# Output projection as seven Strassen block products at the end of a two-attention kernel

## The chip, the cores and the metric

The kernel runs on one core of one Trainium2 chip. The metric is the device time of one execution in microseconds (us). Matmuls run on TensorE (PE), with weight loads as instructions of their own (PEld); elementwise work on VectorE (DVE), ScalarE (ACT) and GpSimd (POOL). DMAs are issued from the queues of SyncE (SP), ACT and POOL.

## The reference

Two attention layers with inputs of their own, A and B, are computed, and their outputs are put side by side. Each has x of 2048 x 1024, wqkv of 1024 x 3072, wo of 1024 x 1024, and 32 heads of 32.

```python
def _A_ref(x, wqkv, wo):      # a query sees 8 keys, 2 positions apart
    W, dil = 8, 2
    idx = pos[:, None] - (jnp.arange(W) * dil)[None, :]
    ...
    attn = _softmax(jnp.where(idx >= 0, logits, -1e9), axis=-1)
    o = jnp.einsum("bhsw,bhswd->bhsd", attn, vg)
    return o.transpose(0, 2, 1, 3).reshape(B, S, D) @ wo

def _B_ref(x, wqkv, wo):      # a query sees the last 256 keys
    scores = jnp.einsum("bhqd,bhkd->bhqk", q, k) * (Dh ** -0.5)
    mask = (idx[:, None] - idx[None, :] >= 0) & (idx[:, None] - idx[None, :] < 256)
    p = _softmax(jnp.where(mask[None, None], scores, -1e9), axis=-1)
    o = jnp.einsum("bhqk,bhkd->bhqd", p, v)
    return o.transpose(0, 2, 1, 3).reshape(B, S, D) @ wo

return jnp.concatenate([a, b], axis=-1)
```

## The kernel before

The work is cut into 8 units of 512 rows: four of B ("dense" units, 0 to 3), then four of A ("window" units, 4 to 7; A's even and odd rows are separated first, so that its dilated window becomes 8 neighbours). A unit has 8 head groups of 4 heads. Units 0, 4 and 6 begin a sequence; the others have a halo of keys from the unit before.

All products keep fp32 accuracy by splitting each operand into a high part (a cast to fp32r) and a low part (what the cast left), and adding three matmuls, high x high, high x low and low x high (`TERMS`). The class `Stream` holds the list of operands that come from DRAM (`items`), 512 KB each: a raw tile is loaded on the POOL queue (`load_to`, L159), cast on DVE or ACT (L201, L204) and its low part made on DVE (L207) by `split_to`. There are `NRAW` raw tiles.

The products run as one ordered list, `gemm`: for each head group the queries and keys (`qk_items`, L518), at certain groups a part of V (`v_items`, L583), at the groups 2 to 5 of a unit the output projection of the unit before (`o_items`, L645, two column blocks of 128 per group), and at the end the projection of unit 7. One column block is 8 x 3 matmuls of 128x512 into one of three PSUM tiles; the result goes out through one staging tile `ost` and ACT's queue.

The attention of a dense head group goes as follows. Queries and keys are copied out of PSUM into `nat` (L455, L459), and SP copies them into one of two stacks, `qst` and `kst` (L479), with the halo from DRAM (L408); the stack of group g is filled again for group g + 2 after the last matmul that reads it. The first pass has 16 score matmuls (L857), each followed by a masked maximum on DVE (L862) and an exponential with its sum on ACT (L867). The logarithms of the sums and the maxima are put into the stack as additional rows (L880 to L902). The second pass has the transposed scores (L940), the exponential (L947), masks on POOL or DVE (L926, L929), and the products with V (L987). The first pass of a group runs between the instructions of the second pass of the group before. A window group has one pass (L711 to L774). In the end `finish` (L822, L826) copies a group's output out of PSUM as a high and a low part; ten such tiles (`NO`) wait for the projection.

The order of the instructions is fixed when the kernel is built: a planner with a clock of its own (`Clock`) gives each instruction of DVE, ACT, POOL and SP a duration, and at each step puts the item on PE that can start first, the second pass ahead of the first and both ahead of `gemm`. A callback can be put off to a planned time (`ck.defer`). Every engine then runs its instructions in the planned order and waits on semaphores for what it needs.

## Time and profile before

| | |
|---|---|
| median of 3 runs | 1830.61 us (1827.76 to 1834.19) |
| profiled execution, first to last instruction | 1830.6 us |
| granted TensorE clock, mean | 0.999 |
| PE busy | 1807.8 us, 14826 matmuls |
| DVE, ACT, POOL busy | 1202.9, 889.4, 394.4 us |
| DMA | 257.43 MB, 141 GB/s in the mean |

Busy time is the time in which an engine's instructions run, without the sequencer's own (waits, DMA issues). Matmuls overlap, so their mean duration in a group's row is longer than the time that one takes from the next; that price is read from a stretch of many in a row. A group's row gives, in this order, line, engine, operation, out<-in, shapes, count, then busy time and mean ns of one, then the engine's idle time ahead of them and what ended it.

### The profile page before, as it was taken

Reading aid. Unit: us, or ns where it says so; the run is one execution under the profiler, and the core shown is the slowest. Engines: PE = TensorE matmul, PEld = TensorE weight load, DVE = VectorE, ACT = ScalarE, POOL = GpSimd, SP = SyncE. Lnnn points to the kernel's source line nnn. Section 1 sums busy time; section 2 is a strip of 40 time slices with the busy share of each in tenths; the row PEclk is TensorE's granted clock in tenths of the full one; section 3 lists DMA queues with packets and bytes.
Section 4 is the critical chain, followed back from the end, with each engine's and each line's share of the span. In section 5 each row is a group of like instructions: output and inputs, shape, how many; then the busy total and the mean of one; then the engine's idle time right before and its main releaser. Section 6 shows DMA issues by size and latency. Waiting matters only on the chain.

```text
span 1830.6 us, 38331 instructions
## 1 busy us (share of the span) xinstructions
PE 1807.8 (99%) x14826; PEld 1477.5 (81%) x14826; DVE 1202.9 (66%) x2694; ACT 889.4 (49%) x2254; POOL 394.4 (22%) x926
## 2 busy tenths in 40 slices
PE   9999999999999999999999999999999999999998
PEld 7787777888778888788887788888888788888887
DVE  6677886768867669777777564655547445655463
ACT  5556466565655655656555343433425234423331
POOL 3322323233242324332233200110001000100000
PEclk9999999999999999999999999999999999999999
DMA  8455665545656456455554343444334443534432
GB/s 242 121 138 139 176 164 150 170 121 160 164 155 164 136 151 183 125 157 141 141 142 130 110 135 116 152 143 130 119 115 143 133 138 108 162 107 128 127 104 83
DMA packets 109141, 257.43 MB, mean 141 GB/s; under 512 B 14496, under 2 KB 29856, under 8 KB 108960
## 3 DMA queue, kind: packets, MB, share of 16 engines
q0 software_dynamic: 41760, 152.06, 28.1%
q1 hardware_dynamic: 56832, 83.00, 17.6%
q10 hardware_dynamic: 10368, 19.93, 3.0%
q8 instruction: 117, 1.92, 0.5%
q14 instruction: 64, 0.52, 0.1%
HBM read 164.63 MB, written 23.07 MB: 103 GB/s over the span
## 4 chain that ended last, share of the span: by engine, by line
PE 92%; DVE 4%; DMA 2%; ACT 2%; issue 1%; SPq 0%; ACTq 0%; POOL 0%; DVEq 0%; POOLq 0%
PE g L518 37%; PE g L645 19%; PE g L583 17%; PE s L940 5%; PE s L857 5%; PE o L987 5%; PE s L711 2%; PE o L774 2%; DMA raw<-xs 1%; DVE w L207 1%; DVE s L862 1%; ACT s L867 0%; DMA qst<-nat 0%; DMA pbuf<-nat 0%; DVE x L207 0%
## 5 line engine op out<-in xcount | busy, mean ns | idle before, releaser
L518 PE MATMUL g<-x,w 128*128 128x512 f32 x3072 | 770.2, 394 | 3.8 <-DVE nm L729 2.4
L518 PEld LDWEIGHTS g<-x,w 128*128 128x128 f32 x3072 | 566.3, 189 | 114.2 <-issue 8.3
L583 PE MATMUL g<-w,x 128*128 128x256 f32 (+1 forms) x2304 | 391.9, 320 | 0.9 <-issue 0.7
L207 DVE TENSOR_TENSOR w<-raw,w 128x512 fp32r<-128x512 f32 x516 | 338.6, 698 | 52.0 <-ACT w L201 44.8
L583 PEld LDWEIGHTS g<-w,x 128*128 128x128 f32 x2304 | 332.3, 190 | 29.2 <-DVE w L207 1.8
L645 PE MATMUL g<-ot,w 128*128 128x512 f32 x1416 | 343.6, 393 | 3.7 <-DVE ot L826 1.8
L867 ACT ACTIVATE s<-s,nm 128x384 f32<-128x384 f32 (+2 forms) x512 | 274.3, 536 | 102.1 <-DVE nm L862 101.8
L862 DVE CUSTOM_DVE_ANT_0 s<-s,mask_d 128x384 f32<-128x384 f32 (+2 forms) x512 | 261.5, 553 | 88.2 <-PE s L857 87.5
L645 PEld LDWEIGHTS g<-ot,w 128*128 128x128 f32 x1416 | 262.4, 188 | 59.3 <-DVE ot L826 3.2
L926 POOL TENSOR_SCALAR_AFFINE_SELECT pbuf<-pbuf 128x128 f32<-128x128 f32 (+1 forms) x606 | 219.8, 391 | 325.1 <-ACT pbuf L947 323.8
L947 ACT ACTIVATE pbuf<-s 128x384 f32<-128x384 f32 (+2 forms) x480 | 202.7, 505 | 72.2 <-PE s L940 70.2
L159 POOL DMA_DIRECT2D raw<-wqk x126 | 68.1, 540 | 457.5 <-DVE w L207 356.3
L204 DVE CAST w<-raw 128x1024 fp32r<-128x1024 f32 x205 | 141.7, 691 | 24.8 <-PE g L518 24.0
L940 PEld LDWEIGHTS s<-qst,kst 128*128 128x128 f32 x704 | 113.0, 188 | 41.2 <-ACT s L867 16.3
L857 PE MATMUL s<-kst,qst 96*128 96x384 f32 (+2 forms) x512 | 142.4, 342 | 0.9 <-ACT s L867 0.6
L940 PE MATMUL s<-qst,kst 128*128 128x256 f32 (+2 forms) x704 | 136.5, 302 | 3.5 <-ACT s L867 3.0
L719 DVE TENSOR_TENSOR band<-s,near 128x160 f32<-128x160 f32 x128 | 32.4, 315 | 158.0 <-PE s L711 158.0
L536 ACT COPY ost<-g 128x512 f32<-128x512 f32 x54 | 31.7, 587 | 207.1 <-PE g L645 200.4
L857 PEld LDWEIGHTS s<-kst,qst 96*128 96x128 f32 x512 | 93.4, 189 | 26.2 <-issue 4.7
L826 DVE TENSOR_TENSOR ot<-o,ot 128x512 fp32r<-128x512 f32 x64 | 44.0, 688 | 101.6 <-ACT ot L822 101.4
L867 ACT ACTIVATION_READ_ACCUMULATOR s<-s,nm 128x1 f32 x512 | 105.3, 206 | 0.0
L159 POOL DMA_DIRECT2D raw<-wo x64 | 34.2, 534 | 304.2 <-DVE w L207 260.2
(77 smaller groups left out, 1298.6 us busy)
## 6 DMA issues: line engine op xcount, KB each, us to landing
raw<-wqk POOLq DMA_DIRECT2D x126, 512.0 KB, 4.3
raw<-wv POOLq DMA_DIRECT2D x72, 512.0 KB, 5.1
raw<-wo POOLq DMA_DIRECT2D x64, 512.0 KB, 4.1
qst<-nat SPq DMA_DIRECT2D x96, 256.0 KB, 5.3
kst<-nat SPq DMA_DIRECT2D x96, 256.0 KB, 5.6
raw<-xs POOLq DMA_DIRECT2D x28, 512.0 KB, 4.6
outs<-ost ACTq DMA_DIRECT2D x56, 256.0 KB, 2.3
kst<-halo SPq DMA_DIRECT2D x72, 128.0 KB, 4.5
```

The costliest lines, as they stand in the source:

```text
L159: (self.nc.scalar if early else self.nc.gpsimd).dma_start(raw if len(ap.shape) == 2 else raw.rearrange("p (a b) -> p a b", a=2), ap)
L204: nc.vector.tensor_copy(t[:, 0, :], raw)
L207: nc.vector.tensor_tensor(t[:, 1, c:c + 512], raw[:, c:c + 512], t[:, 0, c:c + 512].bitcast(F32), op=ALU.subtract)
L518: nc.tensor.matmul(h["ps"], h["w"][:, a, k * P:(k + 1) * P], xt[u][k][:, b, :], start=(k == 0 and i == 0), stop=(k == NK - 1 and i == 2))
L583: nc.tensor.matmul(ps, xt[u][kw * g + k][:, a, p0:p0 + P], h["w"][g][:, c, k], start=(first and t == 0 and half == 0), stop=(last and t == 2),
L645: nc.tensor.matmul(h["ps"], w[:, a, c:c + P], ot[u, k][:, b, :], start=(k == 0 and i == 0), stop=(k == NK - 1 and i == 2))
L857: nc.tensor.matmul(ps[:, :n], q[0:96, j, b * P:(b + 1) * P], kk[0:96, j, c0:c1], start=True, stop=True)
L862: nc.vector.tensor_tensor_reduce(ps[:, :n], ps[:, :n], mask[:, cut:full], scale=-1.0, scalar=BIG, op0=ALU.add, op1=ALU.min, accum_out=nm)
L867: nc.scalar.activation(ps[:, :n], ps[:, :n], AF.Exp, bias=nm, scale=-1.0, accum_out=sm)
L926: nc.gpsimd.affine_select(w, w, pattern=[[0, m], [step, n]], compare_op=ALU.is_ge, fill=0.0, base=base, channel_multiplier=chan)
L940: nc.tensor.matmul(ps[:, i * n:(i + 1) * n], kk[:, j, 256 + kb * P:256 + (kb + 1) * P], q[:, j, q0:q0 + n], start=True, stop=True)
L947: nc.scalar.activation(w, ps[:, :pack * n].rearrange("p (j n) -> p j n", j=pack), AF.Exp)
```

## The change

Two neighbouring units (1024 rows) and the 1024 columns are each taken as 2 x 2 blocks, and so is `wo`; the eight block products of a pair are replaced by seven (Strassen's scheme in Winograd's form). Each product is 4 column blocks of 4 x 3 matmuls. All of it stands at the end of `gemm`.

The attention output of a group no longer stays in SBUF: `finish` copies it once as fp32 into one of two tiles, and SP stores it in DRAM (`od`). The sums of blocks that Strassen needs are made by background tasks: SP loads two blocks of 512 KB into one tile, POOL makes four sums, SP stores 1 MB to DRAM (`sd` for the attention outputs, `td` for `wo`). There are 8 tasks for the two weights, from a planned time of 120 us on, and 4 for each pair after its last group; one task is planned to end before the next begins. The operands of the products are items of the stream like the others, loaded on POOL's queue; an item that needs a sum or an output is held back until the planner's clock says that it has landed (`gates`).

```diff
-NRAW, NP, NO, NS = 3, 768, 10, 4
+NRAW, NP, NS = 4, 768, 4
-O_SLOTS = {2: (0, 1), 3: (2, 3), 4: (4, 5), 5: (6, 7)}
+PRODUCTS = (("11", "11"), ("12", "21"), (0, 3), (2, 2), ("22", 1), (3, 0), (1, "22"))
+BG_FROM, BG_REST, BG_SLACK = 120.0, 8.0, 3.0
-NX, NST, NN = 9, 1, 3
+NX, NST, NN = 9, 2, 3
...
         while self.loaded < min(n, len(self.items)):
+            gate = self.gates.get(self.loaded)
+            if gate and not gate():
+                return
...
-            if u and s in O_SLOTS:
-                plan += [("o", u - 1, n) for n in O_SLOTS[s]]
...
-    plan += [("o", U - 1, n) for n in range(NG)]
+    plan += [("o", v) for v in range(U // 2)]
...
+    od = [dram.tile([P, NG, S], F32, name=f"od{u}") for u in range(U)]
+    sd = [dram.tile([P, 4, 4, S], F32, name=f"sd{v}") for v in range(U // 2)]
+    td = [dram.tile([P, 4, 4, S], F32, name=f"td{ly}") for ly in range(2)]
...
+    def o_parts(v):
+        ly = units[2 * v][0]
+        for i, (a, b) in enumerate(PRODUCTS):
+            for j in range(2):
+                key = ("o", v, i, "s", j)
+                if isinstance(a, str):
+                    u, c = 2 * v + int(a[0]) - 1, 4 * (int(a[1]) - 1) + 2 * j
+                    item(key, "xw", od[u][:, c:c + 2, :])
+                    gates[where[key]] = landed("ot", u * NG + c, u * NG + c + 1)
+                else:
+                    item(key, "xw", sd[v][:, a, 2 * j:2 * j + 2, :])
+                    gates[where[key]] = landed("s", (v, 2 * j), (v, 2 * j + 1))
+            for j in range(2):
+                key = ("o", v, i, "t", j)
+                if isinstance(b, str):
+                    n, c = 4 * (int(b[1]) - 1) + 2 * j, S * (int(b[0]) - 1)
+                    item(key, "w", wo[ly, n:n + 2, :, c:c + S].rearrange("n p c -> p n c"))
+                else:
+                    item(key, "w", td[ly][:, b, 2 * j:2 * j + 2, :])
+                    gates[where[key]] = landed("t", (ly, 2 * j), (ly, 2 * j + 1))
...
+        def run(i, n, k):
             if k == 0:
+                h["ps"], h["b"] = rg.take()
+            w, x = held["o", v, i, "t", n // 2][0], held["o", v, i, "s", k // 2][0][k % 2]
+            c = S * (n % 2) + P * k
+            for t, (a, b) in enumerate(TERMS):
+                nc.tensor.matmul(h["ps"], w[:, a, c:c + P], x[:, b, :], start=(k == 0 and t == 0),
+                                 stop=(k == 3 and t == 2))
+            if k == 1:
+                at = where["o", v, i, "t", 1] + n
+                if at < len(st.items):
+                    st.split_to(at + 1)
...
+            if i == 0:
+                h["a", n] = new("a")
+                nc.scalar.copy(h["a", n], ps)
+                e = ck.use("act", 0.485, ck.now + ck.SEM)
+            elif i == 1:
+                o = stp.tile([P, S], F32, tag="ost", name="ost")
+                e = add(o, h["a", n])
+                store(0, 0, o, e)
...
+            elif i == 5:
+                e = add(h["c", n], h["c", n])
+                store(1, 1, h["c", n], e)
+                e = add(h["a", n], h["a", n])
+            else:
+                e = add(h["a", n], h["a", n])
+                store(0, 1, h["a", n], e)
+            rg.give(bank, e)
...
+    def background():
+        if bg["busy"] or not bg["tasks"]:
+            return
+        bg["busy"] = True
+        loads, ops, dst, key, who = bg["tasks"].pop(0)
+        t = bgp.tile([P, 4, S], F32, tag="bg", name="bg")
+        for c, ap in loads:
+            if len(ap.shape) == 2:
+                ap = ap.rearrange("p (a b) -> p a b", a=2)
+            nc.sync.dma_start(t[:, c:c + 2, :], ap)
+            e = ck.copy("load", ck.now)
+        def step(n):
+            to, x, y, op = ops[n]
+            nc.gpsimd.tensor_tensor(t[:, to, :], t[:, x, :], t[:, y, :], op=op)
+            e = ck.use("pool", 1.2, ck.now)
+            ck.defer(e + BG_SLACK, (lambda: step(n + 1)) if n < 3 else finish)
+        def finish():
+            nc.sync.dma_start(dst, t)
+            e = ck.copy("load", ck.now)
+            def end():
+                done[key][who] = ck.now
+                bg["busy"] = False
+                st.load_to(st.wanted)
+                background()
+            ck.defer(e + BG_REST, end)
+        ck.defer(e + BG_SLACK, lambda: step(0))
...
+    ck.defer(BG_FROM, weight_sums)
...
     def finish(u, s, h):
-        o = opool.tile([P, 2, S], F32R, tag="ot", name="ot")
-        nc.scalar.copy(o[:, 0, :], h["o"])
...
-            nc.vector.tensor_tensor(o[:, 1, :], h["o"], o[:, 0, :].bitcast(F32), op=ALU.subtract)
...
+        o = otp.tile([P, S], F32, tag="ot", name="ot")
+        nc.scalar.copy(o, h["o"])
+        e = ck.use("act", 0.485, ck.now + ck.SEM)
+        ro.give(0, e)
+        def store():
+            nc.sync.dma_start(od[u][:, s, :], o)
+            e2 = ck.copy("store", e)
+            def end():
+                done["ot"][hg] = ck.now
+                st.load_to(st.wanted)
+                if s == NG - 1 and u % 2:
+                    output_sums(u // 2)
+            ck.defer(e2 + 1.0, end)
+        ck.defer(e, store)
```

More of the change, by code (lines that the diff above doesn't have):

```diff
@@ L139, in __init__ @@
         self.raw, self.tiles, self.ready = {}, {}, {}
[L140 removed]
+        self.loaded = self.split = self.wanted = 0
+        self.gates = {}
         self.light = light
@@ L178, in split_to @@
             self.load_to(i + 1)
+            if i not in self.raw:
+                return
             raw, t0 = self.raw.pop(i)
@@ L269, with landed @@
     unit_x(0, 2, 3)
+    od = [dram.tile([P, NG, S], F32, name=f"od{u}") for u in range(U)]
+    sd = [dram.tile([P, 4, 4, S], F32, name=f"sd{v}") for v in range(U // 2)]
+    td = [dram.tile([P, 4, 4, S], F32, name=f"td{ly}") for ly in range(2)]
+    done = {}
+    for k in ("stack", "v", "o", "ot", "nat", "second", "clear", "scores", "s", "t"):
+        done[k] = {}
+    gates = {}
+    def landed(key, *which):
+        return lambda: all(done[key].get(w, ck.now + 1) <= ck.now for w in which)
+    def o_parts(v):
[18 more added lines that the diff above has]
+                    gates[where[key]] = landed("t", (ly, 2 * j), (ly, 2 * j + 1))
     for p in plan:
@@ L354 @@
     halo = [[dram.tile([P, 2, 256], F32, name=f"halo{i}_{s}") for s in range(NG)] for i in range(2)]
-    xt, xready, ot, rows = {}, {}, {}, {}
-    done, waiting = {}, {}
-    for k in ("stack", "v", "o", "ot", "out", "nat", "second", "clear", "scores"):
-        done[k] = {}
+    xt, xready, rows, waiting = {}, {}, {}, {}
     class Ring:
@@ L764, in values_ready @@
         def values_ready():
-            if hg >= NO and ((hg - NO) // NG, NG - 1) not in done["out"]:
-                return None
             return latest(done["v"].get((u, vp)), h.get("p"), ro.when())
```

136 lines of the change are left out of this document (74 added, 62 removed).

## The prediction

> **What bounds the kernel now.** I read the head of the page and its chain first.
>
> ```profile
> span 1830.6 us, 38331 instructions
> ...
> PE 1807.8 (99%) x14826; PEld 1477.5 (81%) x14826; DVE 1202.9 (66%) x2694; ACT 889.4 (49%) x2254; POOL 394.4 (22%) x926
> ...
> PE 92%; DVE 4%; DMA 2%; ACT 2%; issue 1%; SPq 0%; ACTq 0%; POOL 0%; DVEq 0%; POOLq 0%
> ```
>
> PE is busy for 99% and 92% of the chain that ended last runs through it; no other engine passes 66%. So PE's work looks like the price of everything. But a mean over stages hides what the removed matmuls do at their place, so I asked for stretches: unit 0 in its second half, where no output projection runs yet; units 1 to 3, where it is mixed in; a stretch of the window units; the last two minutes.
>
> ```profile
> 137.80:241.90 104.10, 99.03 (x593) 77.72 (x592) 83.47 (x233) 59.19 (x189) 32.50 (x78) 1.00 0.61 165
> 245.00:1026.00 781.00, 777.63 (x4791) 630.66 (x4790) 578.76 (x1460) 456.78 (x1303) 240.01 (x601) 1.00 0.54 148
> 1140.00:1200.00 60.00, 60.00 (x660) 50.45 (x660) 40.78 (x68) 29.79 (x57) 8.92 (x15) 1.00 0.49 147
> 1680.00:1740.00 60.00, 57.62 (x735) 49.23 (x734) 26.99 (x47) 19.23 (x35) 4.23 (x8) 1.00 0.37 115
> 1740.00:1800.00 60.00, 58.88 (x684) 49.08 (x683) 35.53 (x58) 22.67 (x44) 5.29 (x10) 1.00 0.34 101
> ```
>
> Columns are the stretch, its length, busy time of PE, PEld, DVE, ACT, POOL, the granted clock, the DMA share and GB/s. In units 1 to 3 PE lacks only 3.4 us of 781; the window units have PE full with DVE at 68%; but in the unit without projection PE lacks 5.1 us of 104 with DVE at 80%. That points to the attention, so I looked at who holds its copies back: SP's waits inside units 1 to 3.
>
> ```profile
> SPq L408 <- PE s L940: 306.2, 22, 20.5
> SPq L479 <- PE s L940: 220.5, 22, 18.5
> ```
>
> SP brings a head group's keys and queries into one of two buffers, and 527 us of its waits are for the second-pass score matmuls (L940) of the group two before, the last reader of that buffer. PE never starves only because the in-order product stream has something else to run meanwhile. The start of each group's first pass (L857) shows the pace; these are rows of PE's timeline, for groups 4, 8, 9, 13, 17 and 25 (counted from 0; groups 0 to 7 have no halo).
>
> ```profile
> 137.78 0.34 PE L857 MATMUL s<-kst,qst 96*128 96x128 f32 x2
> ...
> 241.90 0.52 PE L857 MATMUL s<-kst,qst 96*128 96x384 f32 x2
> ...
> 268.16 0.51 PE L857 MATMUL s<-kst,qst 96*128 96x384 f32 x2
> ...
> 395.06 0.56 PE L857 MATMUL s<-kst,qst 96*128 96x384 f32 x2
> ...
> 528.28 0.34 PE L857 MATMUL s<-kst,qst 96*128 96x384 f32 x1
> ...
> 785.03 0.34 PE L857 MATMUL s<-kst,qst 96*128 96x384 f32 x1
> ```
>
> Groups 9 to 25: (785.03 - 268.16)/16 = 32.3 us each. Groups 4 to 8, without projection and halo: 26.0 us each, PE at 95%. Groups 13 to 17, where the V products of one unit and the next lie and no projection: 33.3 us each.
>
> **The change part by part.** *Fewer product matmuls.* Before, 64 groups of 8 x 3 = 1536; after, 4 pairs x 7 products x 4 column blocks x 4 x 3 = 1344, of the same 128x512 form. Their clean price is in the chain by time, at the very end:
>
> ```profile
> 1805.13 21.77 PE g L645 x96
> ```
>
> 21.77/96 = 226.8 ns, so 192 fewer are 43.5 us less. This is the whole gain of the arithmetic.
>
> *All of it moved behind the attention.* The last unit's gaps (2.4 + 1.1 us in the two rows above) get a filler that waits for nothing of that unit: -3.5 us. The window units keep PE full at DVE 68%; losing 5.4 us of product per group takes with it the splits of its weights and the low half of its output, so I cost them at nothing; if that cover fails, 1% of what remains of their 779 us (from 1026 to the 1805.13 above, less 4 x 43.5) would be 6 us, kept for the range. The attention output now leaves through two tiles and a store to DRAM; a tile is wanted again two groups later, over 50 us, so that store costs no wait but its SP issue, counted below.
>
> *The dense units lose their filler.* Of the 32.3 us per group, 24 x 0.2268 = 5.4 us are projection. Bound by PE, with today's gaps, a group would take 26.9 us. The question is whether the attention can keep that pace with two buffers. Groups 4 to 8 show 26.0 us, with the copies held by L940, but without halo. What the halo adds per group:
>
> ```profile
> L867 ACT ACTIVATE s<-s,nm 128x384 f32<-128x384 f32 x448 | 249.1, 557 | 85.2 <-DVE nm L862 84.8
> L867 ACT ACTIVATE s<-s,nm 128x256 f32<-128x256 f32 x32 | 14.4, 450 | 3.9 <-DVE nm L862 3.9
> L867 ACT ACTIVATE s<-s,nm 128x128 f32<-128x128 f32 x32 | 10.9, 340 | 13.0 <-DVE nm L862 13.0
> L947 ACT ACTIVATE pbuf<-s 128x512 f32<-128x512 f32 x112 | 65.1, 610 | 19.8 <-PE s L940 18.7
> L947 ACT ACTIVATE pbuf<-s 128x256 f32<-128x256 f32 x112 | 39.8, 396 | 15.4 <-PE s L940 15.1 <-POOL pbuf L926 0.2
> ```
>
> First pass: four 256s and four 128s become 384s, 4 x 0.107 + 4 x 0.217 = 1.3 us. Second pass: two more of 512 and two of 256, 2.0 us. A buffer's cycle is the first pass (the second pass of the group before runs interleaved with it, so it grows by 3.3 us), the logarithms, the second pass (2.0 us more), and the refilling. With two buffers the pace grows by half of 5.3: 26.0 + 2.65 = 28.65 us. The refilling does not shrink with PE's load, it is SP and landing:
>
> ```profile
> 202.16 0.44 PE L940 MATMUL s<-qst,kst 128*128 128x128 f32 x2
> ...
> 202.69 2.73 SPq L479 DMA_DIRECT2D qst<-nat  x3
> ...
> 216.25 0.34 PE L857 MATMUL s<-kst,qst 96*128 96x128 f32 x2
> ```
>
> 13.6 us pass from the last reader to the first use. Bounds: 26.9 from below (PE), 33.3 from above (the V stretch). I take 28.65, nearer to the stretch without projection, because the V work, bunched now, can run ahead by up to two groups once nothing else stands in the product stream. Cost: 24 x (28.65 - 26.9) = +42 us; bounds 0 and +154.
>
> *What is added to these units.* 24 background tasks (12 of them in units 0 to 3): each two to three DMA issues on SP for 2 MB, and four Pool sums of 128x512; and one output store per group on SP. SP's issues stand ahead of the key copies, Pool's sums ahead of the masks (L926) and the weight loads (L159); a sum that waits for a late load holds both, and a load that waits for the single background tile holds the key copies. An SP issue takes 0.6 to 0.9 us (three took 2.73 us above); some three more per group, half of them in the refilling, are about 1 us there, 0.5 us per group: 12 us as upper bound, 0 as lower. No Pool sum is in the trace; from its masks,
>
> ```profile
> L926 POOL TENSOR_SCALAR_AFFINE_SELECT pbuf<-pbuf 128x128 f32<-128x128 f32 x440 | 141.1, 351 | 166.3 <-ACT pbuf L947 165.8
> L926 POOL TENSOR_SCALAR_AFFINE_SELECT pbuf<-pbuf 128x256 f32<-128x256 f32 x166 | 79.9, 495 | 158.8 <-ACT pbuf L947 157.9
> L926 POOL TENSOR_SCALAR_AFFINE_SELECT pbuf<-pbuf x606: 282/293/917, 52.1 to 1030.4; 128x128 f32<-128x128 f32 x110, 128x256 f32<-128x256 f32 x42
> ```
>
> 144 ns per 128 columns give 0.78 us for one input of 512 and 1.6 us for two: 48 in the dense units are 38 to 77 us of an engine that is 31% busy there. Against that, the masks' longest is 917 ns at a median of 293, so a Pool instruction can be held for about one DVE instruction, and DVE, now the busiest after PE, may be held likewise. I take 8 us for all of this, between 0 and 20. The Trainium skill, SBUF — State Buffer, "SBUF: two separate sides", says that Pool and a DVE instruction with two SBUF inputs take a shared port in turns, each holding it for the whole instruction. By that rule each sum would hold up one split, 38 to 77 us of DVE time in units 0 to 3 if every one met a split, and all of it on the path would stand in place of my 8; the mask's row of 917 ns agrees, and no run shows a two-input sum yet.
>
> *The new end.* 28 products of 48 matmuls, 10.9 us each, 305 us in all, now without attention beside them. Per product there are four 512 KB loads, four tiles to split, and four (once eight) additions out of PSUM.
>
> ```profile
> L207 DVE TENSOR_TENSOR w<-raw,w 128x512 fp32r<-128x512 f32 x516 | 338.6, 698 | 52.0 <-ACT w L201 44.8
> L826 DVE TENSOR_TENSOR ot<-o,ot 128x512 fp32r<-128x512 f32 x64 | 44.0, 688 | 101.6 <-ACT ot L822 101.4
> L201 ACT CAST w<-raw 128x1024 fp32r<-128x1024 f32 x52 | 54.1, 1047 | 10.9 <-PE g L583 6.4 <-ACT ost L536 2.7 <-DVE band L731 0.7
> q0 software_dynamic: 41760, 152.06, 28.1%
> q10 hardware_dynamic: 10368, 19.93, 3.0%
> raw<-wqk POOLq DMA_DIRECT2D x126, 512.0 KB, 4.3
> raw<-wv POOLq DMA_DIRECT2D x72, 512.0 KB, 5.1
> pbuf<-xs ACTq DMA_DIRECT2D x2, 512.0 KB, 8.5
> ```
>
> DVE: 8 x 0.698 + 4 x 0.688 = 8.3 us (11.1 in the sixth) of 10.9, casts on ACT. DMA: q0 moved 152 MB in 28.1% of the span, 296 GB/s while it moved, so 2.1 MB take 7.1 us; the stores at q10's 363 GB/s 1.7 us more; the 2 KB rows of half the weight blocks (like wv's, 0.8 us slower) 0.2 us on average: 9 of 10.9. A staging buffer cycles in 0.5 + 4.3 to 5.1 + 1.05 + 1.4 = about 8 us, and four of them must do four loads in 10.9: it fits by 3 us. Were landing 8.5 us, as in the crowded first microseconds, it would miss by 0.6 us per product, 17 us. I take 8, bounds 0 and 30.
>
> Sum, against the profiled execution's span of 1830.6 us (the median of the runs is 1830.61): - 43.5 - 3.5 + 42 + 8 + 8 = +11, **1841.6 us**.
>
> **Rivals.** *PE stays the bound (0.33).* If the passes shorten once PE is less crowded, so that the attention keeps 26.9 us, the 42 us vanish: 1799.6, and 1783.6 without the other two terms. For it: attention goes first when ready, and the V work can fill gaps up to two groups ahead; it decides at 28.2 us per group, below which the change gains. Against it: the 13.6 us of refilling, and PE's 5% of gaps in unit 0.
> *The two cancel (0.10).* A pace of 28.0 to 28.4 us lands within 5.5 us (0.3%, about what a measurement of this kernel can tell from no change).
> *The end is bound by its loads (part of the slower case).* If landing rises to 12 us, a product takes 15/4 x 4 = 15 us in place of 10.9, 115 us more; below 7.9 us it costs nothing. At 83% of the DMA engines' time I give it 0.07; with a third of it, 1880.
> *The change does not do what it says.* The last pair's sums can start only when the attention has ended; four tasks one after another must end within three pairs, 229 us. Two loads, four sums of under 1.6 us and a store come to 9 + 3 + 4 x 4.6 + 8.5 + 8 = 47 us a task even with landing at 8.5 us and the pauses of 3 and 8 us written in the code, 188 us for four, so no wait.
>
> **How the numbers follow.** Attention-bound pace, slower: 0.57, its own range 1836 to 1875 (28.4 to 30 us per group). PE-bound, faster: 0.33. Between: 0.10. The range reaches from the PE-bound case with half of its other terms, 1792, to a pace of 30 us with both added terms near their upper bounds: 1830.6 - 47 + 74 + 12 + 20 = 1890.
>
> **What would show it.** Right: 1344 matmuls at 227 ns behind the attention; starts of the first pass in units 1 to 3 some 28 to 29 us apart; PE idle a few per cent there, its idle ended by ACT and DVE of the scores, SP waiting for L940 as long as now; the end about 313 us. Wrong: first passes 27 us apart, or the end far above 320 us with PE waiting for the splits, or gaps in the window units.

## The result, and the profile after

The changed kernel takes 1907.47 us (median of four runs, 1906.36 to 1908.05) against 1830.84 for the kernel before on the same chip: a ratio of 1.0415, 95% interval 1.040 to 1.043, slower by 77 us. The prediction was 1841.6, between 1792 and 1890. The profiled spans are 1906.0 and 1830.6, so 75.4 us are to be found. The head of the page after, its clock row and its chain:

```profile
span 1906.0 us, 38871 instructions
...
PE 1838.0 (96%) x14634; PEld 1468.7 (77%) x14634; DVE 1338.9 (70%) x2843; ACT 945.3 (50%) x2330; POOL 550.3 (29%) x1039
...
PEclk9998999899988999989999999999999999999999
...
PE 15%; DMA 1%; DVE 0%; issue 0%; ACT 0%; DVEq 0%
PE g L692 15%; DMA outs<-ost 1%; DVE ost L705 0%; DVE w L215 0%; PE o L906 0%; DVE a L705 0%; ACT wide L895 0%; DVEq L705 0%
```

PE has 192 matmuls fewer and is busy 30 us longer; its share fell from 99% to 96%, and the clock row shows a mark below 9 in several slices of the first half. The chain covers only the end part; it cannot price the attention here. Stages can. The last copy of an attention output (tile ot) ends the dense units (first 32 groups) and the window units (last 32); the last two numbers before the semicolon are first and last start. Kernel before, then after:

```profile
L822 ACT CAST ot<-o x32: 585/587/589, 69.2 to 1031.3; 128x512 fp32r<-128x512 f32 x32
L822 ACT CAST ot<-o x32: 585/587/590, 1056.6 to 1794.7; 128x512 fp32r<-128x512 f32 x32
```

```profile
L953 ACT COPY ot<-o x32: 576/587/606, 71.5 to 1004.6; 128x512 f32<-128x512 f32 x32
L953 ACT COPY ot<-o x32: 567/587/591, 1031.4 to 1603.1; 128x512 f32<-128x512 f32 x32
```

The stages of before still hold projection matmuls, so those are taken out at 226.8 ns each. The projection's rows of before say how many lie in the dense units, and the group in the window units; the row of after says what the end started early:

```profile
L645 PE MATMUL g<-ot,w x597: 387/389/502, 260.1 to 1029.1; 128*128 128x512 f32 x199
...
L518 PE MATMUL g<-x,w 128*128 128x512 f32 x1440 | 338.9, 392 | 2.4 <-DVE nm L729 2.4
L645 PE MATMUL g<-ot,w 128*128 128x512 f32 x799 | 189.1, 392 | 3.2 <-DVE ot L826 1.3 <-DVE band L719 1.2 <-ACT ot L822 0.7
```

```profile
L557 PE MATMUL g<-x,w 128*128 128x512 f32 x1398 | 335.0, 396 | 7.1 <-ACT w L209 3.2 <-issue 2.4 <-ACT wide L892 1.4
...
L692 PE MATMUL g<-x,w 128*128 128x512 f32 x34 | 8.5, 399 | 1.5 <-ACT w L209 1.5
```

- Arithmetic: 192 x 0.2268 = -43.5.
- Dense units: before 1031.3 - 597 x 0.2268 = 895.9, after 1004.6: +108.7.
- Window units: before 763.4 - 799 x 0.2268 = 582.2, after 598.5 - 34 x 0.2268 = 590.8: +8.6. The group of the input products says that this is too kind: after has 42 fewer of them in this stretch (1398 against 1440), done ahead in the gaps of the dense units. That is 9.5 us, so like for like the window units lost 18 us and the dense units 99.
- End: 1906.0 - 1603.1 less 1310 x 0.2268 is 5.8; before, 1830.6 - 1794.7 less 140 x 0.2268 is 4.1: +1.7.

The sum is 75.5. So more than the whole loss is in the dense units. Windows of after (columns as in the prediction): second half of unit 0, three stretches of units 1 to 3, the end.

```profile
137.00:242.00 105.00, 99.27 (x541) 74.45 (x541) 78.96 (x211) 56.32 (x182) 45.18 (x90) 0.93 0.63 185
242.00:500.00 258.00, 247.25 (x1450) 190.43 (x1449) 196.11 (x493) 147.78 (x431) 100.91 (x200) 0.96 0.67 192
500.00:785.00 285.00, 272.72 (x1619) 210.21 (x1618) 208.00 (x544) 172.56 (x500) 104.28 (x223) 0.95 0.60 173
785.00:1031.00 246.00, 236.19 (x1665) 183.39 (x1668) 167.16 (x424) 136.46 (x385) 76.34 (x178) 0.97 0.49 134
1600.00:1906.00 306.00, 300.89 (x1358) 247.57 (x1356) 228.48 (x346) 113.10 (x163) 81.92 (x121) 1.00 0.81 264
```

PE shows 94 to 96% busy in the dense stretches, with a clock of 0.93 to 0.97. The number of matmuls is the better measure: 5.6 a microsecond from 242 to 500, where before had 6.1 from 245 to 1026. VectorE, the next, stays at 68 to 76% there. This is an attention that waits for itself. Its pace, as first passes of groups 8, 9 and 25 in PE's timeline:

```profile
255.68 0.51 PE L995 MATMUL s<-kst,qst 96*128 96x384 f32 x2
...
280.70 0.51 PE L995 MATMUL s<-kst,qst 96*128 96x384 f32 x2
...
771.51 0.52 PE L995 MATMUL s<-kst,qst 96*128 96x384 f32 x2
```

Groups 9 to 25 take (771.51 - 280.70)/16 = 30.7 us each: faster than the 32.3 of before, but not by the 5.4 us of projection that left them. Group 8 starts at 255.7, where before had it at 241.9: 13.8 us are lost before unit 1 begins. SP's waits over the whole run still name the second-pass scores (L1078, L940 before) for both copies, though with 357 us they are fewer than the 527 that units 1 to 3 alone had before. New is that PE waits for ScalarE's exponential (L1005) before the next score matmul of a first pass, that is, for a score bank to come free; before, this was 0.6 us in all. The end's chain by time is nearly solid matmul:

```profile
SPq L447 <- PE s L1078: 204.3, 20, 18.2
SPq L518 <- PE s L1078: 152.6, 15, 25.1
```

```profile
PE s L995 <- ACT s L1005: 14.5, 26, 1.3
```

```profile
1642.72 6.45 DMA outs<-ost
...
1686.60 7.12 DMA outs<-ost
...
1695.19 206.70 PE g L692 x910
```

206.70/910 = 227.1 ns a matmul: the products at the end cost what they were said to cost.

### The profile page after: what moved, and what is told of

It is laid out like the page before. It is cut to its first block, busy times and chain, and to the rows that moved or that the text cites. A ratio compares the mean times of both kernels' runs of the same rounds, so it can differ in the third digit from the quotient of the medians.

```text
span 1906.0 us, 38871 instructions
## 1 busy us (share of the span) xinstructions
PE 1838.0 (96%) x14634; PEld 1468.7 (77%) x14634; DVE 1338.9 (70%) x2843; ACT 945.3 (50%) x2330; POOL 550.3 (29%) x1039
## 5 line engine op out<-in xcount | busy, mean ns | idle before, releaser
L557 PE MATMUL g<-x,w 128*128 128x512 f32 x3072 | 779.9, 399 | 9.8 <-ACT w L209 3.8
L557 PEld LDWEIGHTS g<-x,w 128*128 128x128 f32 x3072 | 573.2, 191 | 126.9 <-issue 8.5
L215 DVE TENSOR_TENSOR w<-raw,w 128x512 fp32r<-128x512 f32 x510 | 351.0, 730 | 41.6 <-ACT w L209 35.6
L1005 ACT ACTIVATE s<-s,nm 128x384 f32<-128x384 f32 (+2 forms) x512 | 274.9, 539 | 120.7 <-DVE nm L1000 117.9
L692 PE MATMUL g<-x,w 128*128 128x512 f32 x1344 | 306.2, 390 | 2.2 <-ACT w L209 1.5
L692 PEld LDWEIGHTS g<-x,w 128*128 128x128 f32 x1344 | 251.7, 188 | 56.4 <-DVE w L215 2.3
L995 PE MATMUL s<-kst,qst 96*128 96x384 f32 (+2 forms) x512 | 158.9, 373 | 18.5 <-ACT s L1005 14.5
L212 DVE CAST w<-raw 128x1024 fp32r<-128x1024 f32 x173 | 129.6, 749 | 46.9 <-PE g L557 35.8
L1078 PEld LDWEIGHTS s<-qst,kst 128*128 128x128 f32 x704 | 114.0, 193 | 57.5 <-ACT s L1005 19.8
L1078 PE MATMUL s<-qst,kst 128*128 128x256 f32 (+2 forms) x704 | 146.9, 317 | 7.8 <-ACT pbuf L1085 3.5
L767 POOL TENSOR_TENSOR bg<-bg 128x512 f32<-128x512 f32 x96 | 127.9, 1333 | 22.6 <-DMA bg<-od 20.8
L209 ACT CAST w<-raw 128x1024 fp32r<-128x1024 f32 (+1 forms) x83 | 86.0, 1039 | 91.9 <-DMA raw<-td 31.5
L215 DVE TENSOR_TENSOR x<-raw,x 128x512 fp32r<-128x512 f32 x172 | 121.5, 736 | 9.5 <-ACT x L209 7.8
L209 ACT CAST x<-raw 128x512 fp32r<-128x512 f32 x124 | 70.8, 619 | 84.9 <-DVE ost L705 29.9
```

Source lines behind the costliest of these rows:

```text
L209: nc.scalar.copy(t[:, 0, :], raw)
L212: nc.vector.tensor_copy(t[:, 0, :], raw)
L215: nc.vector.tensor_tensor(t[:, 1, c:c + 512], raw[:, c:c + 512], t[:, 0, c:c + 512].bitcast(F32), op=ALU.subtract)
L557: nc.tensor.matmul(h["ps"], h["w"][:, a, k * P:(k + 1) * P], xt[u][k][:, b, :], start=(k == 0 and i == 0), stop=(k == NK - 1 and i == 2))
L692: nc.tensor.matmul(h["ps"], w[:, a, c:c + P], x[:, b, :], start=(k == 0 and t == 0), stop=(k == 3 and t == 2))
L995: nc.tensor.matmul(ps[:, :n], q[0:96, j, b * P:(b + 1) * P], kk[0:96, j, c0:c1], start=True, stop=True)
```

## The experiments

Theory A: the dense units are bound by the cycle of their buffers (two key/query stacks, four score banks), not by PE, and the background work adds a little. Rivals: the background's sums and loads carry the loss; the halved clock carries it; or the dense units only need filler matmuls. Where a ratio is given, it is to the kernel before, with its interval. Four runs have one execution and so no interval: no projection, the third stack and the fifth bank in that kernel, and the full filler. The differences in time that are drawn from them, 17 us and more, are well above the 6 us by which executions of the kernel before differ (1827.76 to 1834.19).

**No projection at all.** The attention output goes straight to the result, and sums, background and products are left out, so its time is that of the attention and its input products alone.

```diff
-    plan += [("o", v) for v in range(U // 2)]
...
-    ck.defer(BG_FROM, weight_sums)
...
-            nc.sync.dma_start(od[u][:, s, :], o)
+            nc.sync.dma_start(outs[ORDER[u], s], o)
```

> The changed kernel without its sums, without its background tasks and without any output projection; each attention output goes by the same SP store straight into the output array, which so holds something else than the reference. What is left is the attention and its products with the filler gone. Theory A (two key buffers pace the dense units: first pass 23 + gap 9 + second pass 14 + refill 15 us = 61 us for two groups, whatever else runs): first passes of groups 9 to 25 still 29.5 to 30.7 us apart, the granted clock in these units still 0.95 to 0.97, the whole about 1600 us. Theory B (the background sums on POOL, their DMAs on SP and the port shared with DVE slow the dense units): the spacing falls to 28.7 us or below, the whole to about 1555 us, DVE's splits back to 698 ns from 730.

```profile
L945 ACT COPY ot<-o x32: 586/587/590, 71.4 to 990.1; 128x512 f32<-128x512 f32 x32
```

The time was 1584.93. The dense units end at 990.1, 14.5 us before those of the changed kernel and 94 us above the 895.9 of before without its projection. The pace of groups 9 to 25 is 30.0 us, as theory A had it. So the background is 14.5 of the 108.7, and the rest is there without it. (For equal work the background is 20.6: this run does 27 more input products in its dense units than the changed kernel, 1702 against 1675, 6.1 us.) Group 8 starts at 243.4, so 12.3 of the 13.8 us lost in unit 0 go with the background.

**A third key/query stack**, in that kernel without projection:

```diff
-    qst = [stackp.tile([P, 4, S], F32R, tag=f"q{i}", name=f"qst{i}") for i in range(2)]
+    qst = [stackp.tile([P, 4, S], F32R, tag=f"q{i}", name=f"qst{i}") for i in range(3)]
...
-                if hg < 2 or hg - 2 in done["second"]:
+                if hg < 3 or hg - 3 in done["second"]:
```

> The run without projection and background, with a third pair of query and key stacks for the dense groups (what it leaves out is the same). Theory A: the refill leaves the cycle, so the spacing of groups 9 to 25 falls to what PE and DVE set, 26.5 to 28 us, the clock rises to 0.99, and the whole is 50 to 90 us below the run with two stacks. If anything but the buffers paces these units (DVE, ACT, the order of the plan, the background): within 15 us of the run with two.

```profile
L945 ACT COPY ot<-o x32: 586/587/592, 71.0 to 950.6; 128x512 f32<-128x512 f32 x32
```

The time was 1546.82, 38 us less, and the pace 29.1 us: the direction of theory A, but under the expected 50 to 90. The refilling is out of the cycle now, yet the first pass grew from 23.4 to 28.5 us (means of groups 9 to 24 in PE's timeline). A second limit showed behind the first.

**A fifth score bank besides.** One PSUM bank is moved from the products (three to two) to the scores:

```diff
-NRAW, NP, NS = 4, 768, 4
+NRAW, NP, NS = 4, 768, 5
```

> The run without projection and background with three stacks, and five PSUM banks for the scores in place of four (two for the products in place of three; what it leaves out is the same). With three stacks the spacing was still 29.1 us, with the first pass itself lasting 28.5. If the four score banks pace the two interleaved passes then: spacing 27.5 or less and the whole 20 us or more below 1545. If DVE and ACT or PE do (DVE busy for 75%, PE 97%): within 8 us, or longer for want of a product bank.

```profile
L945 ACT COPY ot<-o x32: 586/587/595, 72.1 to 907.5; 128x512 f32<-128x512 f32 x32
```

The time was 1520.61, 26 us less. The first pass fell to 22.1 us, the pace to 27.2, and the dense units to 907.5, 43.1 us earlier. PE's wait for a score bank, with three stacks and then with the fifth bank besides, went with it:

```profile
PE s L985 <- ACT s L995: 14.2, 21, 2.0
```

```profile
PE s L985 <- ACT s L995: 2.9, 9, 0.4
```

But not all of the 43.1 us are a gain. The dense units of the two runs did not do the same work; these are their input products up to the last dense output:

```profile
L550 PE MATMUL g<-x,w 128*128 128x512 f32 x1702 | 450.3, 396 | 2.1 <-ACT x L209 1.1 <-ACT w L209 0.6 <-DVE x L215 0.2
```

```profile
L550 PE MATMUL g<-x,w 128*128 128x512 f32 x1609 | 418.0, 397 | 2.4 <-ACT w L209 1.7 <-DVE w L212 0.6
```

With five banks 93 of them, 21.1 us, were left to the window units, which took 607.4 us in place of 590.4. If each run is put on the 1632 input products that the dense units did before, at 226.8 ns each, the background is 20.6 us, the stack 39.5, and the bank 22.0 of 99: about 82 us have a cause that was taken away and measured, and 17 stay. How the 61.5 us divide between stack and bank may depend on the order in which they were given; no run has five banks and two stacks.

**Filler matmuls in the dense units.** The changed kernel with useless products of x tiles, read by nobody, in slots 2 to 5 of units 1 to 3: 288 matmuls (65 us at 226.8 ns), then 576 (131 us).

```diff
+            if u in (1, 2, 3) and 2 <= s <= 5:
+                plan += [("f", u, s)] * 1
```

The second has `* 2`.

> The changed kernel with 96 matmuls of 128x512 put back per dense unit (units 1 to 3, at the places where the projection stood, half as many as stood there), on operands at hand, with a result that nobody reads: 288 matmuls, 65 us of PE. Theory A: PE has this time free, so the whole stays within 8 us of the changed kernel's 1907. Theory C (the half-clock windows are a cost of their own: PE's gaps lower its clock, and the slower matmuls lengthen the attention): the clock rises to 0.99 and the whole falls by 10 to 30 us, although work is added. If PE's work were the bound: 65 us more.

> The same with 192 matmuls per dense unit, as many as the projection had: 576, 131 us of PE. Theory A: the dense units return to PE's bound, 32.3 us per group as in the kernel before, so some 1.6 us x 24 = 40 us more than the changed kernel, 1945, not 131 more. Theory C: the same pace of 32.3 and a clock of 1.0.

```profile
L974 ACT COPY ot<-o x32: 576/587/593, 71.6 to 1029.1; 128x512 f32<-128x512 f32 x32
```

```profile
L974 ACT COPY ot<-o x32: 576/587/591, 73.3 to 1053.5; 128x512 f32<-128x512 f32 x32
```

The times were 1932.47 (ratio 1.0544, 1.0523 to 1.0565) and 1950.06. The half filler was not free as theory A expected: 65 us of it cost 25. The full one came near what theory A had, 1945: 131 us cost 43 (in whole time; 24.5 and 48.9 at the end of the dense units). So roughly two thirds of the filler fall into time in which PE had nothing; that the rest delays the passes, because one PE with one order serves both, is argued. The same holds for the change read backwards: 135 us of projection taken out of the dense units shortened them by 1031.3 - 1004.6 = 27 us with the background added, and by 1031.3 - 990.1 = 41 without it. The mean clock rose from 0.977 to 0.986 and 0.994, and the time did not fall as the rival of the halved clock has it; as the filler is work of its own, a small gain under its cost is not excluded.

**Idle matmuls on a zero tile**, wherever the plan leaves PE idle for over 0.45 us, 199 in all:

```diff
+        if idle_for > 0.45 and ended > 60.0 and rg.when() is not None and rg.when() <= ended:
+            ps, bank = rg.take()
+            count = int(idle_for / CG)
+            for i in range(count):
+                nc.tensor.matmul(ps, spare[:, :P], spare, start=True, stop=True)
```

> The changed kernel with idle matmuls of 128x512 (zeros into a free product bank, read by nobody) only where the plan leaves PE idle for over 0.45 us and a product bank is free: 199 of them, 45 us of PE time. Nothing else is added. Theory C (half-clock windows cost time by themselves, the measured 89 us of them up to 44 us): the clock rises from 0.977 to 0.985 or more and the whole falls by 10 us or more below 1907. Theory A (the attention's cycle sets the pace; the lower clock only fills time that PE has free): within 8 us of 1907, clock higher.

```profile
core 0: 1917.0 us, clock 0.987
```

```profile
L953 ACT COPY ot<-o x32: 576/587/593, 71.3 to 1010.3; 128x512 f32<-128x512 f32 x32
```

1920.19, ratio 1.0492 (1.0466 to 1.0518): 13 us longer at a higher clock, outside what either theory had. The clock in these traces is either whole or one half, so a mean of 0.977 over 1906 us is 2 x 0.023 x 1906 = 88 us at half speed, and 0.987 over 1917 us is 50. The Trainium skill, TensorE: Matmul & The Clock Gate, "HAM oscillation — how this bites in real kernels", prices throttled time at the half of it that is lost; by an estimate from that, the 38 us fewer would be worth -19 us. The run gave +13, so no price of the half clock shows in the time. The idle matmuls also moved the plan's order, so a small gain under that cost is not excluded.

**No Pool sums.** The background's loads and stores stay, its 96 sums go, so the tiles are stored unsummed:

```diff
-            nc.gpsimd.tensor_tensor(t[:, to, :], t[:, x, :], t[:, y, :], op=op)
```

> The changed kernel without the 96 sums on POOL; the background tasks load and store as before, so the operands of five products of seven hold copies in place of sums. The run without any background ended its attention 24 us earlier. If the sums do that (POOL ahead of the masks and weight loads, or the port shared with DVE): 15 to 25 us below 1907. If the tasks' DMAs do it (SP's queue ahead of the key copies, 4 MB per pair more traffic): within 8 us of 1907.

The group that is taken away, in the changed kernel:

```profile
L767 POOL TENSOR_TENSOR bg<-bg 128x512 f32<-128x512 f32 x96 | 127.9, 1333 | 22.6 <-DMA bg<-od 20.8
```

```profile
L952 ACT COPY ot<-o x32: 586/587/606, 73.4 to 999.2; 128x512 f32<-128x512 f32 x32
```

1904.91, ratio 1.0406 (1.0385 to 1.0428), 2.5 us less than the changed kernel, which the two intervals do not tell from no change. The dense units end 5.4 us earlier, the last attention output comes 8.5 us earlier, and the end takes most of that back. So 128 us of Pool work cost next to nothing in the whole. They do hold up the splits on DVE; this is the group of the weights, in the changed kernel and without the sums:

```profile
L215 DVE TENSOR_TENSOR w<-raw,w 128x512 fp32r<-128x512 f32 x510 | 351.0, 730 | 41.6 <-ACT w L209 35.6
```

```profile
L215 DVE TENSOR_TENSOR w<-raw,w 128x512 fp32r<-128x512 f32 x510 | 333.8, 696 | 50.2 <-ACT w L209 44.2
```

The same 510 splits take 17 us less, and the time hardly moves.

**The background later**, from 1010 us on, when the dense units are through:

```diff
-BG_FROM, BG_REST, BG_SLACK = 120.0, 8.0, 3.0
+BG_FROM, BG_REST, BG_SLACK = 1010.0, 3.0, 3.0
...
-        if bg["busy"] or not bg["tasks"]:
+        if bg["busy"] or not bg["tasks"] or ck.now < BG_FROM:
```

> The changed kernel with all background tasks put off until a planned time of 1010 us, after the dense units (pause after a task 3 us in place of 8, so that they still end in time). If the tasks delay the dense units: last dense output at 985 to 992 us as in the run without background (990.1), in place of 1004.6. The window units then carry 24 tasks in place of 12: if a task costs the same anywhere, 0.8 us each, the whole stays within 8 us of 1907; if only the score passes of the dense units feel it, the whole falls by 12 us or more.

```profile
L953 ACT COPY ot<-o x32: 586/587/590, 72.2 to 988.4; 128x512 f32<-128x512 f32 x32
```

```profile
PE g L692 <- ACT w L209: 79.5, 3, 45.2
```

The dense units ended where expected (988.4), but the time was 1987.45 (1.0847, 1.0819 to 1.0876), outside both cases: products waited 79.5 us for sums that came too late. Less that wait it is 1908, no better than the changed kernel: the window units, which now carry the tasks, took 607.7 us (988.4 to 1596.1) in place of 598.5.

**The plain projection kept in the dense units**, seven products only for the window pairs at the end (768 + 672 = 1440 matmuls, 96 saved, 21.8 us); then the same with shorter pauses between the last pair's sums (0.5 to 1.5 us in place of 3, and 3 in place of 8):

```diff
+            if 1 <= u <= U // 2 and s in O_SLOTS:
+                plan += [("p", u - 1, n) for n in O_SLOTS[s]]
...
-    plan += [("o", v) for v in range(U // 2)]
+    plan += [("o", v) for v in range(U // 4, U // 2)]
```

> A version that keeps the plain projection of the four dense units at its old places (units 1 to 4, output kept in SBUF) and takes the seven products for the two window pairs alone, at the end: 1024 + 672 = 1440 matmuls less 0, that is 768 + 672. By theory A the dense units are back at 32.3 us per group and lose nothing; the window units without filler lose about 9 us (588.7 us from the last dense to the last window output without projection, where 580 would be PE's bound) and the background 4 to 6; 96 matmuls fewer are -21.8, the filled end -3.5: 1820, between 1812 and 1828. If the loss came from the end or from DRAM round trips, it would stay above 1835.

> The version with plain projection in the dense units and seven products for the two window pairs at the end came out at 1856: from the last attention output (1676) to the end it took 178 us with PE busy for 124 of 154, since the last pair's sums start only there and only one pair of products covers them. Here the pauses of these four tasks are cut (0.5 and 3 us in place of 3 and 8). If that wait was the cause, 20 to 25 us go: 1830 to 1836, no better than the kernel before. If not: 1850 or more.

```profile
1700.00:1854.00 154.00, 123.58 (x536) 101.16 (x534) 92.87 (x137) 42.20 (x60) 40.70 (x52) 0.92 0.67 226
```

```profile
1760.00:1790.00 30.00, 10.76 (x46) 8.52 (x45) 9.41 (x13) 3.96 (x7) 11.32 (x12) 0.73 0.60 211
```

1855.73 (1.0133, 1.0113 to 1.0154) and 1852.23 (1.0107, 1.0084 to 1.0129); 1812 to 1828 and 1830 to 1836 were expected. The first missed because PE stood for 30 us of the last 154 (columns as above): the last pair's sums can only begin when the attention ends, and one pair of products before it is too short a cover. The second missed because the pauses were not what makes these sums long: PE still stood for 19 of 30 us, and the last of the four sums was stored only 3.5 us sooner. These are its two stores on SP, first version, then second:

```profile
1783.16 0.88 SPq L839 DMA_DIRECT2D sd<-ot  x2
```

```profile
1779.62 0.88 SPq L840 DMA_DIRECT2D sd<-ot  x2
```

What holds the tasks in their place is open. The dense units did take what they took before (pace 32.25 us). In the changed kernel three pairs lie ahead, and this wait does not exist.

**The changed kernel with the third stack**, complete. The stack takes the space of the sums, and the products of the last three pairs use the score banks.

```diff
-        buf = s % 2
+        buf = hg % 3 if dense else s % 2
...
+        ring = rs if v else rg
```

> The whole changed kernel with a third pair of key and query stacks for the dense groups (its space is that of the product sums, which are wanted only later; the products of the last three pairs take the score banks of PSUM). Without projection and background the third stack moved the end of the dense units from 990.1 to 950.6 us. If the cycle of two stacks is part of the cause in the changed kernel itself: last dense output at 960 to 970 us in place of 1004.6, spacing of groups 9 to 25 at 29.0 to 29.7 in place of 30.7, the whole 1865 to 1880. If the background in the dense units takes the place of the freed wait: within 10 us of 1907.

1864.27 (1.0173, 1.0147 to 1.0198): 43 us less, just past the expected 1865 to 1880, with the dense units through at 962.5 and a pace of 28.8 us.

**And with the fifth score bank as well** (pauses between sums 1.5 us; what the pauses alone do was not tried):

```diff
-NRAW, NP, NS = 4, 768, 4
+NRAW, NP, NS = 4, 768, 5
...
-BG_FROM, BG_REST, BG_SLACK = 120.0, 8.0, 3.0
+BG_FROM, BG_REST, BG_SLACK = 120.0, 8.0, 1.5
```

> The changed kernel, complete, with a third key/query stack and a fifth score bank at once (the product stream is left with two banks until the end, the pause between two background sums is 1.5 us in place of 3). Theory A (the loss sits in the buffers of the dense units, and products at the end cost what their matmuls cost): the third stack alone gave 1864.3; the fifth bank took 43 us from the dense units of the kernel without projection and gave 17 of it back in the window units, so this run comes to 1864 - 26 = about 1838, between 1828 and 1850, with the last dense attention output near 920 us, the pace of groups 9 to 25 between 27.2 and 28.5 us, and the end about 300 us. Theory B (the way through DRAM, its sums and its stores are the larger price and cap the gain): 1855 to 1870, dense units ending above 940 us. If A is right the change is at best near break-even with the kernel before, because 43.5 us are all that it can give.

```profile
L955 ACT COPY ot<-o x32: 585/586/589, 70.3 to 905.9; 128x512 f32<-128x512 f32 x32
```

```profile
905.90:1531.00 625.10, 601.28 (x7802) 496.91 (x7802) 382.65 (x617) 257.85 (x498) 105.20 (x139) 0.99 0.50 160
```

```profile
L556 PE MATMUL g<-x,w 128*128 128x512 f32 x1464 | 351.8, 398 | 8.0 <-ACT vbuf L574 4.6 <-ACT w L209 1.6 <-DVE vbuf L577 1.2
```

1838.8 (ratio 1.0053, 1.0036 to 1.0069), 69 us less than the changed kernel and within a microsecond of what theory A expected. That it fits so closely is partly luck: the dense units end at 905.9 in place of 920, and the window units and the end take about as much longer. 905.9 is 10 us above the clean 895.9. What is left is in the window units: 625.1 us in place of 598.5. Part of it can be counted: 1464 input products lie there, 66 more than in the changed kernel, 15 us. The dense units did less ahead; whether for want of gaps or of the third product bank, the runs do not separate.

**The fifth bank lent to the products in the window units**, whose attention takes four score banks at a time:

```diff
+    rg3, rs4 = Ring(psg, ["g0", "s4", "g1"]), Ring(psg, ["s0", "s1", "s2", "s3"])
...
+        ring = rg3 if WIN(u, s) else rg
```

> As the run before (third key/query stack, five score banks, quick sums), but the fifth score bank is lent to the products of the window units, whose attention takes four banks at a time: they have three product banks again, as in the changed kernel, from the fifth key/query column block of the first window unit on. In the run before the dense units ended at 905.9 us, and the window units took 625.1 us (905.9 to 1531.0) in place of 598.5 in the changed kernel, 26.6 more. Theory A (two product banks are the whole of that): the window units take about 600 us again, the last attention output comes near 1508, and the kernel about 1838.8 - 25 = 1814, between 1808 and 1822, which is faster than the kernel before by 0.4 to 1.2 %. Theory B (the window units lose because the dense units leave them less work done ahead, or because of background work that falls into them now): they stay at 620 us or more and the time at 1833 to 1842.

```profile
911.50:1530.70 619.20, 595.58 (x7802) 495.75 (x7803) 377.85 (x613) 264.13 (x502) 105.42 (x139) 0.99 0.50 161
```

1839.45 (1.0044, 1.0032 to 1.0056). No gain: the window units are 6 us shorter, the dense units 5.6 us longer. Two product banks in the window units are not what they lose by. PE idles 23.6 us here (619.20 - 595.58) as against 7.4 of 763.4 in the window units of before, with DVE at 61%. None of these kernels beat the kernel before; whether that one would itself gain from a third stack and a fifth score bank was not tried.

## Why the prediction was wrong in size

**Fewer product matmuls, -43.5:** right, at 227.1 ns each.

**The end, +8 less 3.5 for the filled stall:** right in kind, +1.7 measured. Loads, splits and additions kept up with the products at a DMA share of 0.81 (four fifths of the engines' time, where the working had 9 of 10.9 us); the two pauses in the chain are for output tiles. The rival of an end bound by loads did not occur, and neither did a wait for the last sums, whose cover of three pairs held.

**Window units at nothing:** wrong, though only 8.6 us show. PE full and DVE at 68% were read from 60 us of this stage as a cover that needs no projection. Over the whole stage PE already lacked 7.4 us before, and it lacked 19.8 after:

```profile
1031.30:1794.70 763.40, 756.02 (x8543) 629.80 (x8544) 430.66 (x723) 287.90 (x537) 75.40 (x137) 1.00 0.43 130
```

```profile
1004.60:1603.10 598.50, 578.70 (x7736) 481.84 (x7737) 379.90 (x610) 256.68 (x494) 103.12 (x136) 0.99 0.52 163
```

Per equal work they lost 18 us in the changed kernel, and 20 in the run with three stacks and five banks without projection (907.5 to 1514.9 is 607.4, against 582.2 + 24 x 0.2268 = 587.6). The bound of 6 us was too low.

**The dense units' pace, 28.65 us:** the step that failed. The term "the dense units lose their filler", +42 us, was sized too small: 30.7 us per group were measured, 30.0 without background, and 24 x (30.7 - 26.9) is 91 us. Its base was too low. The starts of groups 4 to 9 before are 20 to 32 us apart, so the mean depends on where it is taken: from group 4 to 8 it is the 26.0 that was used, from group 5 to 9 it is 27.7. The parts of the cycle of groups 4 to 7 (first pass, gap, second pass, refill), 19.7 + 7.5 + 13.5 + 13.0 us, add to 53.7 over two buffers, or 26.85. With 2.65 for the halo that is 29.5, already past the 28.2 at which the change breaks even. The halo part came out right in its sum and not in its parts: in the run without projection the cycle is 54.7 us for groups 4 to 7 and 60.1 for groups 9 to 24, 5.4 more where 5.3 was worked out, but the first pass grew by 3.7, the gap by 1.7 and the second pass by 1.0, and the refill shrank by 1.0, where 3.3, 0, 2.0 and 0 were worked out. The four score banks, the second limit, were never in the working. PE waits for one in the changed kernel, and with a third stack the first pass is 28.5 us long until a fifth bank brings it to 22.1; how much of the 30.7 is theirs no run shows by itself. So the mechanism of the likeliest case held, and its place, but not its size; the rival that PE stays the bound did not come about until both limits were gone.

The upper bound of 33.3 us was misread too: groups 13 to 17 were said to run without projection, but 48 of its matmuls lie between the two starts, 10.9 us or 2.7 per group:

```profile
L645 PE MATMUL g<-ot,w x48: 387/393/501, 513.6 to 528.1; 128*128 128x512 f32 x48
```

**The miss in the dense units, added up:** 24 groups at 30.7 - 28.65 are 49 us. Group 8 was 13.8 us late already, nearly all of it background, for which the sum had 8 in all dense units. Together 49 + 13.8 - 8 are 55 of the 58.7 us by which the dense units missed (108.7 against 42 + 8).

**Background, +8 between 0 and 20:** 14.5 at the end of the dense units, inside its bounds, though the 20.6 for equal work are just past the upper one; most of it falls in unit 0. The sums are not its main part: without them the dense units end 5.4 us earlier. A sum takes 1.33 us, between the 0.78 and 1.6 worked out. By the rule quoted from the Trainium skill, SBUF — State Buffer, "SBUF: two separate sides", each sum could have held up one split, 38 to 77 us of DVE time for the 48 sums of the dense units. The trace agrees in kind, with splits of 730 ns beside the sums and 696 without, but that is 17 us over 510 splits of the whole run, and the 5.4 us at the end of the dense units are far below the rule's upper case.

**Where the expected gain went, then:** the 43.5 us arrive in full at the end; 108.7 are lost where the filler was taken away (99 for equal work). Two stacks and four banks had been enough only as long as 135 us of projection gave PE something to do during their cycle. With both limits lifted the change comes to 0.5% above before. What remains there, by spans, is -43.5 + 10 in the dense units + 35 in the window units + 3 at the end = 5 us. Of the 35, 10 go with the background (617.4 without its early products against 607.4 in the run without projection), 5 are 24 more input products, and some 20 stay. They fit the cover that the projection gave, but a version that gives the window units products as filler was not tried, so that is argued from the counts, not shown. Another rival stands untested there: SP's one queue now also waits for the attention outputs that it must store (L958), 163 us in the window units of the changed kernel, with other copies behind it.

## What to carry to other kernels

Work that fills another stage's gaps costs much less than its own time where it stands, so removing or moving it must be costed at what its place will do without it: here 135 us of matmuls left the dense units, and these got 27 us shorter, or 41 where no background was added. A pace without the filler is best built as the sum of the parts of one buffer's cycle (pass, gap, pass, refill) over the number of buffers, and each pool on that cycle can be a limit of its own, the PSUM banks as well as the SBUF stacks. When a stage with gaps has other work queued behind it, count the instructions in each stage before comparing stage times: work done ahead makes the next stage look cheaper than it is.

## What the runs showed of the hardware

In the changed kernel the granted clock fell to one half in stretches, most of them in the dense units, in this one with no DMA at all:

```profile
170.70:180.90 10.20, 9.78 (x35) 5.43 (x36) 4.60 (x19) 7.88 (x26) 3.61 (x14) 0.50 0.00 0
```

PE shows 9.78 of 10.20 us busy, with 35 matmuls, 3.4 a microsecond where the kernel before had 6.1 in units 1 to 3. But matmuls take longer at this clock: the six second-pass score matmuls below take 0.48 us each, while the 256 of that form in the kernel before took 0.27 us each (70.0 us in all). So inside such a stretch neither PE's busy share nor the count of matmuls tells a gap from a slow matmul. Gaps show around its start, with what ended them in brackets:

```profile
169.82 0.44 PE L1078 MATMUL s<-qst,kst 128*128 128x384 f32 x1 [0.64 <-DVE qst L1040]
170.84 2.89 PE L1078 MATMUL s<-qst,kst 128*128 128x384 f32 x6 [0.58 <-ACT pbuf L1085]
```

No run shows a price of the half clock in the time: three runs with filler raised the mean from 0.977 to 0.986, 0.987 and 0.994, and all three took longer. Each also added work to PE, so a small price is not excluded.
